# Gated mix of two attentions on one core: another order of the first loads, splits and keys, and borrowed probability buffers kept until the 48th quad

## The chip, the cores and the metric

One core of one Trainium2 chip. The metric is device microseconds of one execution, the median of the runs shown; lower is better. The inputs lie in the chip's memory at the start and the result must lie there at the end.

## The reference

The input x has 2048 tokens of width 512. Two attentions with 32 heads of width 16 are computed from it and mixed by a gate per token. In attention a all heads share one key and one value head; attention b has its own keys and values for each head. Cut to what matters:

```
g = sigmoid((x * gate_w).sum(-1))                      # one number per token
qa = heads(x @ wq); ka = x @ wk; va = x @ wv           # 32 query heads, one key and one value head
a = concat(softmax(qa @ ka.T * 16**-0.5) @ va) @ wo_a
qb, kb, vb = heads(x @ wqkv)                           # 32 heads each
b = concat(softmax(qb @ kb.T * 16**-0.5) @ vb) @ wo_b
out = g * a + (1 - g) * b
```

All is float32. The exponential is needed for 2 x 32 x 2048 x 2048 scores.

## The kernel before

**Tiles.** P = 128 partitions, NT = 16 token tiles of x, which are loaded two at a time as eight pairs (`x_tiles[k]`, k = 0 to 7; "x tile" below means such a pair). The heads of each attention are cut into NG = 4 groups of eight. The groups of a and b take turns (a0, b0, a1, b1, ...), and each group is done in two halves of the queries, each half in two parts of four heads: 32 phases in all. A phase has 32 *quads* of two *scores* each, one for each pair of its heads. So there are 1024 quads and 2048 scores; a score u = 2 x quad + 0 or 1 is a block of 128 x 1024 numbers. Scores 0 to 255 belong to group a0, 256 to 511 to b0, and so on.

**A score's way.** TensorE multiplies keys with queries into a PSUM bank named `sc` (eight matmuls, L623). ScalarE takes the exponential of the bank into a probability buffer in SBUF (L637, out `prob` or another borrowed name). TensorE multiplies the probabilities with the values and adds them up in the PSUM bank `pair[0]` (L678). Keys and queries are held as sums of two float16 numbers ("high part" and "residue"), so that the products keep float32's accuracy.

**Chained quads.** VectorE takes some quads from ScalarE: it computes the exponential by a polynomial, from the bank `pair[1]` (also called `spare`). Each such score is a chain of six instructions on VectorE: convert (L837), mantissa (L840), power (L844) and three steps of the polynomial (L849). Which quads are chained is the set `vector`.

**What sets the order.** The program is written out by a planner while it is built (`plan`): at each step it looks at estimated clocks of the engines (`plan.pe`, `plan.act`, `plan.dve`), at due times and at free buffers, and decides whether TensorE next does a score, a pair of values, or a piece of other work (a *unit*: x turns, products of queries, keys and values for the next group, output products). The estimates are constants at the top of the file, in nanoseconds: `EXP` = 904 for an exponential, `SCORES` = 215, `PRODUCT` = 215, and `X_JOB` = 560 for a quarter of one x tile's turns. A run then simply executes the order that came out; the planner's constants cost no time themselves, but another constant gives another order.

**Buffers.** Six probability buffers (`prob0` to `prob5`) are permanent. At the start the planner also has the SBUF of things that are done with or not needed yet: the first x tiles (`lent`), four buffers of the pool for group b's keys (`early0` to `early3`) and three in group b's value tile (`vB`), the last seven called `borrowed`. When the values of a quad are done, `summed` gives its two buffers back, except borrowed ones from the 16th quad on (`at[0]` is the quad that the next score belongs to):

```
for tile in (probs[2 * m], probs[2 * m + 1]):                          # L687
    if id(tile) in borrowed and at[0] >= 16:                           # L688
        continue
```

**The start.** Before the planner takes over, the work is written by hand. x tiles 0 and 1 are loaded over SyncE's and ScalarE's queues, 2 and 3 over SyncE's, then the query weights (`wqa`) over ScalarE's and behind them three small loads (`gate_w`, `wk`, `wv`, into the buffer `prob`, L289). For each of x tiles 0 to 3, TensorE turns the tile (`x_turns`, L298), ScalarE writes the high part (`x_hi`, L312) and VectorE the residue (`x_lo`, L317) into `xT`. The query weights are split in the same way (`first_w`, L248 on ScalarE and L249 on VectorE), the small weights in two steps on VectorE (`split`, L219 and L220); for each, SyncE's queue then moves a copy with its two halves of 64 rows swapped (`swapped`, L212). The loop before:

```
for k in range(4):                                                     # L1143
    if k == 3:
        banks.append(bank(2))
    x_turns(k, banks[k], TURNS)
    x_hi(k, as_x(banks[k]), nc.scalar)
    if k == 0:
        first_w()
        split(wkv16[0][:, 0], wkv16[0][:, 1], wkv, UP)
        ...
    x_lo(k, as_x(banks[k]))
```

The four x tiles have three banks of their own and `spare`; the first and the fourth share one (`bank(2)` takes the place that the first had). After the loop come the products of the first key tile (`kv_products`, L332, and `halve`, L351 to L356, which split them into high part and residue), then the query products Q of group a0 (L1163), whose high part ScalarE takes (L1167) and whose residue VectorE takes (L1172), and which sixteen transfers (`lay`, L401), eight of them ahead of the first score, move to the tiles `Qa`. The keys are turned by TensorE (`k_turn`, L367) and copied by VectorE into `kA` (`k_put`, L377). Then follow the other key tiles, x tile 4 and the first scores; x tiles 5 to 7 and the other keys come between scores.

## Time and profile before

| | |
|---|---|
| median of 3 runs | 1838.48 us (1838.03 to 1838.57) |
| the profiled execution's own time | 1836.4 us |
| its span | 1834.6 us |
| busy share of the span: TensorE (PE) | 95% |
| ScalarE (ACT) | 97% |
| VectorE (DVE) | 71% |
| GpSimd (POOL) | 16% |
| matmuls | 45161 |
| first exponential starts | 27.96 us |
| last exponential starts | 1811.77 us |

Times within an execution are microseconds from the start of the span. The profile names engines PE, PEld (TensorE's weight loads), DVE, ACT, POOL and SP; a "q" behind a name is the queue on which that engine issues DMAs. In a row of the page's groups stand the line, the engine, the operation, what it writes <- what it reads, the count of instructions, then the busy time and the mean nanoseconds of one, then the engine's idle time just ahead of these instructions with what released it. A row of the timeline begins with its start and duration; a bracket at the end holds how long the engine idled ahead of it, and on what. A row of windows has the window and its length, then the busy time with the count of instructions (of one line on its engine, or, where all are asked for, of PE, PEld, DVE, ACT and POOL in this order), and in the last columns the granted TensorE clock, the share of the DMA engines that was busy (over 1 where several packets overlap), and GB/s.

### The profile page before, as it was taken

The page shows a single profiled execution, that of the slowest core. Times are in us where ns is not written, and L with a number is a line of the kernel's source. Part 1 is how long each engine was busy: PE and PEld are TensorE (multiplying, and loading weights), DVE is VectorE, ACT ScalarE, POOL GpSimd, SP SyncE. Part 2 cuts the span into 40 slices and gives each one's busy share as a digit, 9 for nine tenths or more (in the row PEclk, how much of TensorE's full clock was granted, in tenths as well). Part 3 has the DMA queues.
Part 4 walks back from the last instruction along what each step waited for, and adds up shares of the span by engine and source line. Part 5 has one row for each costly group of instructions (what it writes and reads, how often), then busy time and mean ns, then how long its engine had stood idle before and what let it go on. Part 6 is the DMA issues. An engine that isn't in the chain of part 4 may idle for free.

```text
span 1834.6 us, 96600 instructions
## 1 busy us (share of the span) xinstructions
PE 1746.1 (95%) x45161; PEld 847.5 (46%) x45161; DVE 1300.5 (71%) x1465; ACT 1786.2 (97%) x1948; POOL 291.9 (16%) x367
## 2 busy tenths in 40 slices
PE   8999999999999999998999999999999999999896
PEld 5544444444444444444444444444444444444442
DVE  5277656789565776869667656886967567588886
ACT  5999999999999999999999999999999999999995
POOL 2212002121020121311202012132200202112000
PEclk9999999999999999999999999999999999999998
DMA  5121122233131232411313112342211213235211
GB/s 151 36 61 44 51 54 61 77 71 55 32 76 39 55 66 59 89 43 34 55 43 73 32 41 57 78 83 60 50 39 43 55 38 70 54 58 135 49 61 61
DMA packets 64887, 109.45 MB, mean 60 GB/s; under 512 B 14480, under 2 KB 22928, under 8 KB 64480
## 3 DMA queue, kind: packets, MB, share of 16 engines
q0 software_dynamic: 21504, 43.99, 13.0%
q1 hardware_dynamic: 39744, 56.99, 11.2%
q8 instruction: 355, 5.82, 1.3%
q10 hardware_dynamic: 3232, 2.23, 0.4%
q14 instruction: 52, 0.43, 0.1%
HBM read 14.75 MB, written 33.55 MB: 26 GB/s over the span
## 4 chain that ended last, share of the span: by engine, by line
ACT 73%; PE 11%; issue 8%; DVE 7%; DMA 1%; SPq 0%; ACTq 0%; DVEq 0%; POOL 0%
ACT prob L637 73%; PE pair L678 5%; PE sc L623 3%; DVE vec L849 2%; PE pair L207 1%; DVE vec L837 1%; DVE vec L844 1%; DVE sum L517 1%; DVE vec L840 0%; DVE dT L568 0%; PE pair L298 0%; SPq L561 0%; PE pair L1163 0%; PE pair L332 0%; DMA vec<-in_A_x_dram 0%
## 5 line engine op out<-in xcount | busy, mean ns | idle before, releaser
L637 ACT ACTIVATE prob<-sc 128x1024 f32<-128x1024 f32 x1911 | 1757.5, 1127 | 9.2 <-PE sc L623 8.6
L678 PE MATMUL pair<-prob,vA 64*32 64x512 f32 (+1 forms) x8016 | 515.6, 570 | 0.1
L678 PE MATMUL pair<-prob,vB 64*32 64x512 f32 (+1 forms) x7840 | 509.1, 578 | 0.0
L623 PE MATMUL sc<-Qb,K 64*32 64x512 f16 x7632 | 400.4, 380 | 42.8 <-ACT prob L637 32.1
L849 DVE SCALAR_TENSOR_TENSOR vec<-vec,vec 128x1024 f32<-128x1024 f32 x348 | 424.2, 1232 | 3.5
L623 PE MATMUL sc<-Qa,kA 64*32 64x512 f16 x7824 | 406.0, 380 | 17.7 <-ACT prob L637 9.5
L623 PEld LDWEIGHTS <-K 64*32 64x32 f16 x8192 | 201.2, 89 | 421.5 <-issue 383.1
L623 PEld LDWEIGHTS <-kA 64*32 64x32 f16 x8192 | 199.6, 89 | 387.9 <-issue 344.6
L837 DVE TENSOR_SCALAR vec<-pair 128x1024 int32<-128x1024 f32 x116 | 140.9, 1215 | 59.2 <-PE pair L623 59.0
L678 PEld LDWEIGHTS pair<-prob,vA 64*32 64x32 f32 x8016 | 154.9, 105 | 21.3 <-issue 3.1
L678 PEld LDWEIGHTS pair<-prob,vB 64*32 64x32 f32 x7840 | 151.7, 105 | 18.2 <-issue 0.5
L849 DVE SCALAR_TENSOR_TENSOR vec<-vec 128x1024 f32<-128x1024 f32 x116 | 143.3, 1236 | 1.1
L527 POOL DMA_DIRECT2D out_dram<-sum x48 | 60.0, 1250 | 386.4 <-DVE sum L517 359.8
L568 DVE RECIPROCAL dT<-dT 128x256 f32<-128x256 f32 (+1 forms) x66 | 111.4, 1693 | 9.7 <-DMA dT<-raw 9.7
L743 DVE COPY raw<-pair 128x1024 f32<-128x1024 f32 x31 | 37.9, 1222 | 96.8 <-PE pair L678 96.8
L517 DVE TENSOR_SCALAR sum<-pair,gate_up 128x512 f32<-128x512 f32 x112 | 77.7, 735 | 29.4 <-PE pair L207 29.3
L840 DVE TENSOR_SCALAR vec<-vec 128x1024 int32<-128x1024 int32 x116 | 84.5, 728 | 1.6
L844 DVE TENSOR_SCALAR vec<-vec 128x1024 int32<-128x1024 int32 x116 | 85.5, 737 | 0.0
L442 DVE TENSOR_SCALAR hivb<-pair 128x1024 f16<-128x1024 f32 x8 | 9.8, 1225 | 98.3 <-PE pair L207 98.3
L442 DVE TENSOR_SCALAR hiqb<-pair 128x1024 f16<-128x1024 f32 x8 | 9.8, 1225 | 92.0 <-PE pair L207 92.0
L401 POOL DMA_DIRECT2D Qa<-hiqa x31 | 17.6, 568 | 349.9 <-DVE hiqa L442 329.2
L207 PEld LDWEIGHTS <-o 64*32 64x32 f16 x3072 | 51.5, 93 | 39.1 <-ACT o L574 5.7
(160 smaller groups left out, 1253.3 us busy)
## 6 DMA issues: line engine op xcount, KB each, us to landing
out_dram<-sum POOLq DMA_DIRECT2D x48, 512.0 KB, 5.7
vB<-vB SPq DMA_DIRECT2D x16, 384.0 KB, 4.1
dT<-raw SPq DMA_DIRECT2D x32, 128.0 KB, 3.5
oT<-raw SPq DMA_DIRECT2D x32, 128.0 KB, 3.6
out_dram<-sum SPq DMA_DIRECT2D x8, 512.0 KB, 3.3
xT<-out_dram SPq DMA_DIRECT2D x16, 256.0 KB, 4.3
dT<-raw SPq DMA_DIRECT2D x62, 64.0 KB, 2.2
out_dram<-xT SPq DMA_DIRECT2D x12, 256.0 KB, 2.5
```

The source lines that it names most:

```text
L207: nc.tensor.matmul(outs[n : n + COLS, i], lhs[i][rows(i), n : n + COLS], rhs[i][rows(i)], start=start, stop=stop)
L517: nc.vector.tensor_scalar(state["sum"][:, e], pair[1][:, e], g, None, op0=ALU.mult)
L527: done = plan.on_pool([lambda: nc.gpsimd.dma_start(dst, state["sum"], accum_op=ALU.add)], t, 1300)
L568: nc.vector.reciprocal(d[:, c : c + cut], d[:, c : c + cut])
L623: nc.tensor.matmul(bank[a : a + COLS, hh], k[rows(hh), key : key + COLS], Q[src, gi, half, p][rows(hh), j * BLK : (j + 1) * BLK], start=Tr ...
L637: nc.scalar.activation(probs[u], sc, AF.Exp, scale=SCALE / (UP * UP))
L678: nc.tensor.matmul(pair[0][32 * k : 32 * k + 32, i, cols], v[rows(i)], probs[2 * m + k // 2][rows(i), hh, cols], start=first, stop=last)
L743: nc.vector.tensor_copy(state["raw"], full)
L837: nc.vector.tensor_scalar(tile("p").bitcast(I32), pair[1], SCALE / (UP * UP) / math.log(2) * 2.0 ** 23, None, op0=ALU.mult)
L840: nc.vector.tensor_scalar(tile("m").bitcast(I32), tiles["p"].bitcast(I32), 0x7FFFFF, 125 << 23, op0=ALU.bitwise_and, op1=ALU.bitwise_or)
L844: nc.vector.tensor_scalar(tile("w").bitcast(I32), tiles["p"].bitcast(I32), 0x7F800000, 0x40000000 | LEAD, op0=ALU.bitwise_and, op1=ALU.bit ...
L849: nc.vector.scalar_tensor_tensor(p, m if i == 3 else p, VEC[i], m if i else w, op0=ALU.add, op1=ALU.mult)
```

## The change

It has three parts. In the start, ScalarE loads its exponential table ahead of issuing anything else, and the three small loads are issued on GpSimd's queue; each x tile's residue is computed directly behind its high part, with the query weights' split behind the first tile's and the small weights' split behind the second's; all key products come behind Q's, and the copy of the first turned keys is on ScalarE. Borrowed buffers are used until the 48th quad instead of the 16th. And the planner counts 685 ns instead of 560 for a quarter of an x tile's turns.

```diff
@@ constants
-X_JOB = 560
+X_JOB = 685
@@ loads of the small weights
+    nc.scalar.activation(warm, warm, AF.Exp)
     for src, m in parts_kv:
-        nc.scalar.dma_start(wkv[:, :, m], src)
-    nc.scalar.activation(warm, warm, AF.Exp)
+        nc.gpsimd.dma_start(wkv[:, :, m], src)
     nc.vector.memset(stats, 0.0)
     nc.gpsimd.memset(vA[0], 1.0)
     nc.gpsimd.memset(vA[1], 1.0)
@@ copies of turned keys
-    def k_put(h, bank, tiles):
+    def k_put(h, bank, tiles, copy=nc.vector.tensor_copy):
...
-            nc.vector.tensor_copy(to, bank.rearrange("p a q -> p (a q)")[:, at * P : (at + n) * P])
+            copy(to, bank.rearrange("p a q -> p (a q)")[:, at * P : (at + n) * P])
@@ summed
-            if id(tile) in borrowed and at[0] >= 16:
+            if id(tile) in borrowed and at[0] >= 48:
                 continue
@@ start
         x_turns(k, banks[k], TURNS)
         x_hi(k, as_x(banks[k]), nc.scalar)
+        x_lo(k, as_x(banks[k]))
         if k == 0:
             first_w()
+        if k == 1:
             split(wkv16[0][:, 0], wkv16[0][:, 1], wkv, UP)
             swapped(wkv16[1], wkv16[0], nc.sync)
             for i in range(2):
                 x_load(4, i, nc.sync)
-        x_lo(k, as_x(banks[k]))
...
     kn, take, halve, k_top = kv_split(0, pv)
-    kv_products(0, 0, pv, STEPS)
-    halve(slice(0, 1))
     for n, (c, w, a, b) in enumerate(STEPS):
...
     for i in range(2):
         nc.scalar.activation(hilo[0][:, i], spare[:, i], AF.Copy, scale=UP ** -1)
-    turned_k = bank(3)
-    k_turn(kn, turned_k, (0, 4))
-    k_put(0, turned_k, (0, 4))
+    kv_products(0, 0, pv, STEPS)
+    halve(slice(0, 1))
     for i in range(2):
         nc.vector.scalar_tensor_tensor(hilo[1][:, i], spare[:, i], UP ** -1, hilo[0][:, i], op0=ALU.mult, op1=ALU.subtract)
     to = q_tiles("a", 0, 0)
-    moves = ... ((nc.sync, nc.scalar), (nc.gpsimd, nc.sync, nc.gpsimd, nc.scalar)) ...
+    moves = ... ((nc.sync, nc.scalar), (nc.gpsimd, nc.sync, nc.scalar, nc.gpsimd)) ...
     for move in moves[0][:2] + moves[1][:2] + moves[0][2:] + moves[1][2:]:
         move()
-    for i in range(1, 4):
+    kv_products(0, 1, pv, STEPS)
+    turned_k = bank(3)
+    k_turn(kn, turned_k, (0, 4))
+    k_put(0, turned_k, (0, 4), nc.scalar.copy)
+    for i in range(2, 4):
         kv_products(0, i, pv, STEPS)
     halve(slice(1, 4))
     last = bank(4)
```

What the planner makes of it shows at two places. First the start. On ScalarE, the difference of the two orders (a minus is the kernel before, a plus the changed one), with the loads of x and the query weights ahead and the first tile's high part (L312) and the query weights' (L248) behind:

```order
 L238 DMA wqa_133<-in_A_wq_dram 128x4x128
-L289 DMA prob_102<-in_gate_w_dram 128x4x1
-L289 DMA prob_102<-in_A_wk_dram 128x4x16
-L289 DMA prob_102<-in_A_wv_dram 128x4x16
-L290 ACT_TABLE_LOAD
-L290 ACTIVATE warm<-warm 128x1
+L288 ACT_TABLE_LOAD
+L288 ACTIVATE warm<-warm 128x1
 L312 ACTIVATE xT<-pt_146 128x8x128
 L248 ACTIVATE w16qa_135<-wqa_133 128x512
```

The three small loads have left ScalarE's queue, and the table's load has moved up behind the query weights' DMA.

On VectorE at the same place: `pt_146`, `pt_147`, `pair_83` and `pt_223` are the banks of x tiles 0 to 3, `w16qa` the split query weights, `wkv` the split small weights.

```order
 L1142 CAST ident_86<-ident 128x128
+L317 SCALAR_TENSOR_TENSOR xT<-pt_146,xT 128x8x128
 L249 SCALAR_TENSOR_TENSOR w16qa_135<-wqa_133,w16qa_135 128x512
+L317 SCALAR_TENSOR_TENSOR xT<-pt_147,xT 128x8x128
 L219 TENSOR_SCALAR wkv_93<-prob_102 128x132
 L220 SCALAR_TENSOR_TENSOR wkv_93<-prob_102,wkv_93 128x132
-L317 SCALAR_TENSOR_TENSOR xT<-pt_146,xT 128x8x128
-L317 SCALAR_TENSOR_TENSOR xT<-pt_147,xT 128x8x128
 L317 SCALAR_TENSOR_TENSOR xT<-pair_83,xT 128x8x128
 L317 SCALAR_TENSOR_TENSOR xT<-pt_223,xT 128x8x128
```

The residues of the first two x tiles have moved ahead of the small weights' split, the first also ahead of the query weights'.

Second, the end of group b0, scores 503 to 513. On ScalarE of the kernel before (the number behind `sc` is that of the score, the number behind that a running one):

```order
L637 ACTIVATE prob3_100<-sc503_11506 128x1024
L637 ACTIVATE prob1_98<-sc504_11524 128x1024
L637 ACTIVATE prob4_101<-sc505_11543 128x1024
L637 ACTIVATE prob2_99<-sc512_11561 128x1024
L637 ACTIVATE prob3_100<-sc513_11580 128x1024
```

And of the changed kernel:

```order
L637 ACTIVATE prob5_102<-sc505_11335 128x1024
L637 ACTIVATE prob3_100<-sc506_11354 128x1024
L637 ACTIVATE prob4_101<-sc507_11428 128x1024
L637 ACTIVATE prob0_97<-sc512_11446 128x1024
L637 ACTIVATE prob5_102<-sc513_11520 128x1024
```

Before, the scores 506 to 511 are not on ScalarE but chained on VectorE; in the changed order 506 and 507 are exponentials. In the same way 188 and 189, chained before, are exponentials in the changed order; over the whole program 1936 scores stand on ScalarE instead of 1932. From score 503 to about score 1243 each engine of the changed kernel has the rows that stand 512 scores later in the kernel before, and from there to the end it has the same rows at the same score. VectorE of the changed kernel, around score 520 (`raw7` is the copy of a phase's value sums, L475 prepares values of the next group b):

```order
L743 COPY raw7_11551<-pair1_83 128x1024
L475 TENSOR_SCALAR vB0_91<-pair0_82 128x8x2x16
L837 TENSOR_SCALAR vec0_103<-pair0_82 128x1024
L840 TENSOR_SCALAR vec2_105<-vec0_103 128x1024
L844 TENSOR_SCALAR vec1_104<-vec0_103 128x1024
L837 TENSOR_SCALAR vec3_106<-pair0_82 128x1024
L849 SCALAR_TENSOR_TENSOR vec0_103<-vec2_105 128x1024
```

VectorE of the kernel before, around score 1032:

```order
L743 COPY raw15_22069<-pair0_82 128x1024
L475 TENSOR_SCALAR vB0_91<-pair1_83 128x8x2x16
L837 TENSOR_SCALAR vec0_103<-pair1_83 128x1024
L840 TENSOR_SCALAR vec5_108<-vec0_103 128x1024
L844 TENSOR_SCALAR vec3_106<-vec0_103 128x1024
L837 TENSOR_SCALAR vec1_104<-pair1_83 128x1024
L849 SCALAR_TENSOR_TENSOR vec0_103<-vec5_108 128x1024
```

The kinds and their order are the same, with the two PSUM pairs and some scratch buffers exchanged.

2 lines of the change are left out of this document (1 added, 1 removed).

## The prediction

> **What bounds the kernel now.** I read the page first, then the activations by stretches, then the first 28 us.
>
> ```profile
> span 1834.6 us, 96600 instructions
> PE 1746.1 (95%) x45161; PEld 847.5 (46%) x45161; DVE 1300.5 (71%) x1465; ACT 1786.2 (97%) x1948; POOL 291.9 (16%) x367
> ACT 73%; PE 11%; issue 8%; DVE 7%; DMA 1%; SPq 0%; ACTq 0%; DVEq 0%; POOL 0%
> L637 ACT ACTIVATE prob<-sc 128x1024 f32<-128x1024 f32 x1911 | 1757.5, 1127 | 9.2 <-PE sc L623 8.6
> ```
>
> ScalarE's exponentials (L637) are 73% of the chain that ended last, and once they run ScalarE idles for only some 9 us. So the time is: when the first exponential starts, how many there are times their pace, what ScalarE waits in between, and the tail. The windows of line L637 give the pace and the stretches. I cut them at scores 32, 503 and 1243 (the second and third cut are explained below); the activation's place follows from counting the score numbers in ScalarE's order. Each count but the first and the one that starts at 27.95 holds one activation that began ahead of the window.
>
> ```profile
> 27.95:477.10 449.15, 446.01 (x485) 1.00 0.22 55
> 477.10:1120.09 642.99, 639.82 (x697) 1.00 0.26 56
> 920.51:1565.48 644.97, 641.95 (x699) 1.00 0.25 55
> 1120.09:1811.77 691.68, 689.44 (x751) 1.00 0.27 59
> 27.95:58.96 31.01, 30.12 (x32) 1.00 0.24 65
> 58.96:477.10 418.14, 415.89 (x454) 1.00 0.21 54
> 592.53:704.42 111.89, 111.89 (x123) 1.00 0.25 53
> ```
>
> 592.53 to 704.42 has no idle time: 122 activations in 111.89 us, **0.917 us each**. That is what one exponential more or less on ScalarE costs. At this pace the first 32 would take 29.3 us and took 31.0, so 1.7 were lost; the next 453 would take 415.4 and took 418.1, so 2.7 were lost.
>
> **The count.** The page's groups L637 hold 1932 activations; 116 of the 2048 scores go to VectorE (line L837). In ScalarE's order of the changed kernel 1936 scores stand: VectorE has two fewer in the third phase (188 and 189 move to ScalarE) and two fewer in the eighth (506 and 507). So ScalarE gets 4 x 0.917 = 3.67 us more. Two of these can be read as a measured stretch. From score 503 on, the changed kernel does on TensorE, score by score, what the kernel before does 512 scores (one pair of head groups) later, as far as score 1243; from there to the end it does what the kernel before does at the same score. The kernel before took 644.97 us for 1015 to 1755 and 642.99 us for 503 to 1243, waits included: **+1.98 us**. From 1243 on nothing changes: **0**. The scores before 503 are in new order, with two more activations: **+1.83 us**, and their waits are open.
>
> **The beginning.** In the timeline's rows (start, duration, engine, line) ScalarE first, its DMA queue ACTq with it:
>
> ```profile
> 1.66 0.46 ACTq L238 DMA_DIRECT2D wqa<-in_A_wq_dram  x1
> 6.45 1.28 ACT L290 ACT_TABLE_LOAD   x1 [6.45 <-DMA vec<-in_A_x_dram]
> 7.85 1.01 ACT L312 ACTIVATE xT<-pt 128x1024 f16<-128x1024 f32 x1
> 8.76 0.62 ACT L248 ACTIVATE w16qa<-wqa 128x512 f16<-128x512 f32 x1
> 14.46 1.02 ACT L312 ACTIVATE xT<-pt 128x1024 f16<-128x1024 f32 x1 [2.73 <-PE pt L298]
> 20.93 1.08 ACT L1167 ACTIVATE hiqa<-pair 128x512 f16<-128x512 f32 x2 [5.44 <-PE pair L1163]
> 23.37 1.40 ACTq L401 DMA_DIRECT2D Qa<-loqa  x2
> 27.96 1.02 ACT L637 ACTIVATE prob<-sc 128x1024 f32<-128x1024 f32 x1 [1.47 <-PE sc L623]
> ```
>
> VectorE:
>
> ```profile
> 9.41 0.69 DVE L249 SCALAR_TENSOR_TENSOR w16qa<-wqa,w16qa 128x512 f16<-128x512 f32 x1 [4.00 <-ACT w16qa L248]
> 10.70 0.23 DVE L219 TENSOR_SCALAR wkv<-prob 128x132 f16<-128x132 f32 x1 [0.60 <-DMA prob<-in_A_wv_dram]
> 11.18 2.35 DVE L317 SCALAR_TENSOR_TENSOR xT<-pt,xT 128x1024 f16<-128x1024 f32 x2
> 16.66 0.18 DVE L351 TENSOR_SCALAR k<-pair 128x32 f32<-128x32 f32 x1
> 17.11 0.23 DVE L356 TENSOR_TENSOR kn<-k,kn 128x64 f16<-128x64 f32 x1
> 22.05 1.29 DVE L1172 SCALAR_TENSOR_TENSOR loqa<-pair,hiqa 128x512 f16<-128x512 f32 x2 [0.39 <-ACT hiqa L1167]
> 25.79 1.02 DVE L377 CAST kA<-pt 128x384 f16<-128x384 f32 x2 [1.29 <-PE pt L367]
> 27.00 1.22 DVE L317 SCALAR_TENSOR_TENSOR xT<-pt,xT 128x1024 f16<-128x1024 f32 x1
> ```
>
> TensorE, and SyncE's queue:
>
> ```profile
> 5.20 3.71 PE L298 MATMUL pt<-ident,vec 128*64 128x128 f32 x64 [0.38 <-DVE ident L1141]
> 8.75 1.92 PE L298 MATMUL pair<-ident,vec 128*64 128x128 f32 x32
> 12.45 1.97 PE L298 MATMUL pt<-ident,vec 128*64 128x128 f32 x32 [1.79 <-DVE xT L317]
> 14.35 0.77 PE L332 MATMUL pair<-wkv,xT 64*128 64x33 f16 x48
> 15.54 5.36 PE L1163 MATMUL pair<-xT,w16qa 64*128 64x512 f16 x48 [0.42 <-ACT xT L312]
> 20.83 0.30 PE L367 MATMUL pt<-ident,kn 128*64 128x128 f16 x4
> 25.25 0.51 PE L367 MATMUL pt<-ident,kn 128*64 128x128 f16 x12
> 27.48 0.41 PE L623 MATMUL sc<-Qa,kA 64*32 64x512 f16 x8 [1.73 <-DMA Qa<-loqa]
> 10.13 1.21 SPq L212 DMA_DIRECT2D w16qa<-w16qa  x2
> ```
>
> And how long such a swap of a weight's rows takes to land, from the DMA issues (kilobytes each, median us):
>
> ```profile
> w16qa<-w16qa POOLq DMA_DIRECT2D x6, 128.0 KB, 2.4
> ```
>
> The stall to see is TensorE's: the fourth tile's turns, at 12.45, wait 1.79 us for the bank of the first tile, whose residue stands on VectorE (11.18) behind weights that came by DMA at 10.70. Now step by step. ScalarE loads its table at 2.1 instead of 6.45, so the first tile's high part starts when its turns end (half of 5.20 to 8.91, so 7.1) and ends at 8.1. Its residue is first on VectorE: 8.1 to 9.3 (half of 2.35). The weights' residue follows at 9.5 to 10.2; in the kernel before it ended at 10.1, so their swap leaves at the same time, by 10.13 + 1.21 = 11.3, and at 2.4 has landed by 13.7. The fourth tile's turns start when TensorE is free, 8.75 + 1.92 = 10.7, and end at 12.65; its high part on ScalarE ends at 13.7. **The Q products start at 13.7, not 15.54: -1.8**, and end at 19.1. The swap has no room left there; it did land by 15.5 before, since Q waited for L312 and not for a DMA.
>
> Then some is given back. The first tile of keys (0.77), which stood in a gap at 14.35, now runs behind Q, 19.1 to 19.9. Its halving on VectorE (16.66 to 17.34, 0.68) lands between Q and Q's residue: 20.0 to 20.6, then the residue to 21.9, against 23.34. TensorE from 19.9: three more key tiles at 0.77, the turn (0.30), the fifth x tile (1.97) and the other keys' turn (0.51), 25.0 in all against 25.76. These keys' copy on VectorE (1.02) ends at 26.1, and the first score follows at 26.2, against 27.48. Q's residue is no longer last: its moves took from 23.37 to the first score in 27.48, at most 4.1, and 21.9 + 4.1 = 26.0. The second score uses the bank of the fifth x tile, whose residue (1.22, behind the keys' copy, the values and the gate) ended at 28.22 and now ends at 27.5; the second exponential moves from 28.89 to 28.0. I take **-0.85 us** from there, not -1.25 from the first score, since the later one holds.
>
> What is hidden: the keys' copy that moves to ScalarE stands behind Q's moves (1.40, from 21.9 to 23.3) and costs between 0.5 and the 1.08 of L1167; it is done by 24.4, before the bank is turned into again at 24.5. Without that cover it costs what it is late. The three small loads on GpSimd's queue are the first thing there and push two memsets that nobody reads before 26 us. Nothing before Q's last third needs the small weights' split; in VectorE's order it stands ahead of the residues of the third and fourth tile. That third starts at 13.7 + 3.6 = 17.3, two residues take 2.45, so the weights may land at 14.3 instead of 10.7 for nothing.
>
> The first 32 scores lost 1.7 us since TensorE has x turns, key products and values between scores. In the changed order the same work (12 turn jobs, 8 key jobs, 8 pairs of values) stands between 30 scores instead of 28, up to the second keys' turn. A code fetch of TensorE falls in it as well:
>
> ```profile
> 49.23 0.27 PE L332 MATMUL pair<-wkv,xT 64*128 64x33 f16 x8 [0.66 <-issue]
> ```
>
> Two more scores give ScalarE 1.83 us of work there and cost TensorE 2 x 0.41: up to -1.0, with another fetch +0.3. I take **-0.5**.
>
> **The other waits before score 503.** They lost 2.7 us; the largest is of this kind, TensorE at a chained pair's values before VectorE has finished it:
>
> ```profile
> 341.39 2.96 ACT L637 ACTIVATE prob<-sc 128x1024 f32<-128x1024 f32 x3 [1.09 <-PE sc L623]
> ```
>
> Before, those values stood 10 scores behind their products (9.2 us), with 9.2 us of VectorE work ahead of them. The changed order has that place no more, but one with 18 scores (16.5 us) and 16.6 us of work, at score 408. One goes, one comes: **0**, between -1.9 (none) and +2.6 (two more). Keeping the borrowed tiles only moves values later; the last borrowed tile is filled at score 110, and keys are laid there behind score 194, so no queue waits for it.
>
> **The sum.** 1834.6 - 0.85 - 0.5 + 1.83 + 1.98 + 0 = 1837.1, so +2.5 us. The profiled execution's own time was 1836.4 and the median of the runs 1838.48; on the median the forecast is **1840.9 us**. 0.2% (about what a measurement of this kernel can tell from no change) is 3.7 us: faster means under 1834.8, slower over 1842.2.
>
> **The rivals.**
> *A wait that takes the place of the one removed (slower).* The pair at score 408 and the next tight one, at 458 (18 scores, 15.7 us of work), can both make TensorE wait as at 341 us. So can group b's second keys: their last products now stand behind score 276 (before: 250), they are needed at 288, and I work out some 3 us in hand. Then ScalarE loses 1.3 us more for each: one gives 1842.2, two 1843.5. It decides from one more such wait than before. For it: the whole first quarter is new order. Against: the three places have 0 to 3 us in hand. Chance 0.22.
> *The start gives nothing (slower).* The loads are crowded:
>
> ```profile
> 8.00:9.00 1.00, 1.00 (x24) 1.00 (x22) 0.00 (x0) 1.00 (x2) 0.00 (x0) 1.00 1.15 270
> ```
>
> The DMA engines are full. In the kernel before, the small weights were sent behind x and Q's weights; now they are sent among them. At worst Q's weights land when the last small load did, 10.6 instead of 8.7: ScalarE splits them until 11.2, their swap leaves at 11.9 and Q starts 1.1 later. The start is then +0.25, the time 1842.0. [...] Chance 0.10.
> *ScalarE's waits go (no change).* More buffers in the first 96 scores let TensorE run ahead: -1.9 more, 1839.0. It would have to come from waits that are not for buffers (the row at 341 us isn't). Chance 0.10.
> *The four exponentials cost nothing,* where TensorE and not ScalarE is last: 1837.2. Against: the windows show 0.917 in every quiet stretch, and the two for 503 to 1243 are measured. Chance 0.05.
>
> **How the numbers follow.** The forecast has 0.53. The range takes the ends of start, first scores and waits as far as they go together: low 1838.0 (-1.0 in the first 32, -1.9 in waits, and the start as taken), high 1843.8 (two more waits and a start 0.6 worse). Slower over 0.2%: most of the first rival, half of the second and the upper end of the forecast, 0.31. Faster by 0.2% would need 6.1 us beyond the forecast, more than all waits that the changed part has (1.7 + 2.7): 0.03. Within: 0.66.
>
> **What would show it.** The changed profile should show L637 in 1936 activations, the first at 26.7 and the second at 28.0; Q's products at 13.7 with no wait of TensorE for L317 at 12.45; the 33rd activation at about 57.6 (58.97 before); and from score 503 to 1243 some 645 us, from there to the last 691.7. Wrong is the forecast if score 503 starts later than 478.5 or earlier than 475.5 (477.1 - 1.35 + 1.83 = 477.6), or if the later stretches differ by over 1 us from these.

## The result, and the profile after

The changed kernel takes 1844.24 us (median of 7 runs, 1842.63 to 1845.91) against 1838.03 for the kernel before on the same chip; the ratio is **1.0029, 95% interval 1.0020 to 1.0039**, which is +5.3 us where +2.4 was forecast (1840.9 against 1838.48). In a second set of runs it was 1.0036 (1.0022 to 1.0050). The profiled execution took 1845.78 us, its span is 1844.0. That is one of the slower executions of this kernel, as 1836.4 was one of the faster ones of the kernel before, so the two profiles are 9.4 us apart where the medians are 6.2 apart.

The windows of the exponentials' line (L637), cut at the same scores as before (the first exponential, 32, 503, 1243, the last):

```profile
31.30:63.51 32.21, 29.82 (x32) 1.00 0.28 75
63.51:484.23 420.72, 418.10 (x457) 1.00 0.21 53
484.23:1129.44 645.21, 641.66 (x699) 1.00 0.26 55
1129.44:1820.84 691.40, 689.09 (x752) 1.00 0.28 59
```

From score 503 on it is as forecast: 645.21 us to score 1243 ("some 645") and 691.40 from there to the last (691.7). Of the 9.4 us, 3.3 are there at the first exponential (31.30 against 27.96), 1.2 come in the first 32 scores (32.21 against 31.01), 2.6 from there to score 503 and 2.2 to score 1243; behind it -0.3 to the last exponential and +0.3 in the tail. The start was forecast as a gain. VectorE's first instructions, in the kernel before:

```profile
1.31 1.47 DVE L271 TENSOR_SCALAR index<-index 128x1 f16<-128x1 f16 x7
4.86 0.29 DVE L1141 TENSOR_TENSOR ident<-pair,index 128x128 f32<-128x128 f32 x1 [1.94 <-PE pair L1140]
```

And in the changed kernel, with GpSimd's rows of the same time below:

```profile
1.31 3.64 DVE L271 TENSOR_SCALAR index<-index 128x1 f16<-128x1 f16 x7
7.47 0.29 DVE L1141 TENSOR_TENSOR ident<-pair,index 128x128 f32<-128x128 f32 x1 [2.38 <-PE pair L1140]
1.27 0.94 POOL L290 DMA_DIRECT2D prob<-in_gate_w_dram  x1 [0.83 <-POOLq L1446]
2.20 0.77 POOL L290 DMA_DIRECT2D prob<-in_A_wk_dram  x1
2.96 0.75 POOL L290 DMA_DIRECT2D prob<-in_A_wv_dram  x1
```

L271 is a chain of seven tiny instructions that count 0 to 127 into `index`, from which the identity for the turns (L1141) is made. They took 1.47 us and now take 3.64, while GpSimd prepares the three small loads (until 3.7) and then does the two memsets that the loads pushed back (0.54 us each, until 4.7). The third to sixth of the seven take 0.46, 1.05, 0.42 and 0.99 us, where 0.17 is usual. The identity is 2.6 us later. The prediction does not have these rows: it looked at what the loads do to other loads, and not at what VectorE does while GpSimd prepares them.

TensorE from there to the first score, and ScalarE's first exponentials:

```profile
5.01 0.29 PE L1138 MATMUL pair<-level,index 128*128 128x128 f16 x1 [2.37 <-DVE index L271]
7.82 5.26 PE L298 MATMUL pt<-ident,vec 128*64 128x128 f32 x64 [0.38 <-DVE ident L1141]
14.66 1.91 PE L298 MATMUL pt<-ident,vec 128*64 128x128 f32 x32
17.70 5.36 PE L1162 MATMUL pair<-xT,w16qa 64*128 64x512 f16 x48 [1.12 <-ACT xT L312]
26.90 0.57 PE L332 MATMUL pair<-wkv,xT 64*128 64x33 f16 x31 [1.03 <-issue]
27.40 1.97 PE L298 MATMUL pt<-ident,vec 128*64 128x128 f32 x32
30.81 0.41 PE L623 MATMUL sc<-Qa,kA 64*32 64x512 f16 x8 [1.12 <-DVE kA L377]
31.30 1.02 ACT L637 ACTIVATE prob<-sc 128x1024 f32<-128x1024 f32 x1 [0.86 <-PE sc L623]
32.69 3.81 ACT L637 ACTIVATE prob<-sc 128x1024 f32<-128x1024 f32 x4 [0.37 <-PE sc L623]
```

The fourth tile's turns (14.66) follow without the wait of 1.79 us, as forecast. But TensorE idled 2.37 us for the index, and then took 5.26 us for the first two tiles instead of 3.71. In windows of TensorE (length, busy time, count, granted clock):

```profile
7.82:11.02 3.20, 3.20 (x30) 1.00 0.67 202
11.02:13.08 2.06, 2.06 (x42) 1.00 0.00 0
```

The same matmuls run at 0.107 us apiece until 11.02 and at 0.054 from there (38 of the 42 start in the second window). The record of the granted clock begins with a rise to full at 11.02, and at 4.24 in the kernel before; the clock column reads 1.00 ahead of its first record, so the half clock of a start is seen in the counts and not in that column. Q starts at 17.70, not at 13.7: of these 4.0 us some 2.6 are the identity's and 1.5 the clock's. Behind Q, at 26.90, TensorE waits 1.03 us for nothing that the rows show, in the middle of the key products. I take it for a wait for TensorE's own code: in all fourteen profiles listed below, each such wait of 0.5 us or more in the first 60 us ends 2.3 to 2.7 us behind the start of a 16 KB transfer on the instruction queue (here one that starts at 24.39; in the kernel before one at 46.90, ahead of the wait of 0.66 that ends at 49.23).

### The profile page after: what moved, and what is told of

It reads as the page before. It is cut to its first block, busy times and chain, and to the rows that moved or that the text cites. A ratio compares the mean times of both kernels' runs of the same rounds, so it can differ in the third digit from the quotient of the medians.

```text
span 1844.0 us, 96547 instructions
## 1 busy us (share of the span) xinstructions
PE 1750.1 (95%) x45145; PEld 847.1 (46%) x45145; DVE 1273.8 (69%) x1435; ACT 1790.3 (97%) x1954; POOL 295.8 (16%) x370
## 3 DMA queue, kind: packets, MB, share of 16 engines
q0 software_dynamic: 21600, 44.06, 13.5%
q1 hardware_dynamic: 39744, 56.99, 11.1%
## 5 line engine op out<-in xcount | busy, mean ns | idle before, releaser
L637 ACT ACTIVATE prob<-sc 128x1024 f32<-128x1024 f32 x1874 | 1728.3, 1126 | 9.8 <-PE sc L623 8.7
L678 PE MATMUL pair<-prob,vA 64*32 64x512 f32 (+1 forms) x7664 | 505.5, 571 | 0.1
L849 DVE SCALAR_TENSOR_TENSOR vec<-vec,vec 128x1024 f32<-128x1024 f32 x336 | 413.4, 1242 | 3.2
L837 DVE TENSOR_SCALAR vec<-pair 128x1024 int32<-128x1024 f32 x112 | 135.6, 1211 | 58.2 <-PE pair L623 58.0
L678 PEld LDWEIGHTS pair<-prob,vA 64*32 64x32 f32 x7664 | 151.1, 105 | 18.4 <-issue 1.4
L840 DVE TENSOR_SCALAR vec<-vec 128x1024 int32<-128x1024 int32 x112 | 81.1, 724 | 1.3
L844 DVE TENSOR_SCALAR vec<-vec 128x1024 int32<-128x1024 int32 x112 | 80.0, 714 | 0.0
```

The lines of the kernel that those rows point to most:

```text
L637: nc.scalar.activation(probs[u], sc, AF.Exp, scale=SCALE / (UP * UP))
L678: nc.tensor.matmul(pair[0][32 * k : 32 * k + 32, i, cols], v[rows(i)], probs[2 * m + k // 2][rows(i), hh, cols], start=first, stop=last)
L837: nc.vector.tensor_scalar(tile("p").bitcast(I32), pair[1], SCALE / (UP * UP) / math.log(2) * 2.0 ** 23, None, op0=ALU.mult)
L840: nc.vector.tensor_scalar(tile("m").bitcast(I32), tiles["p"].bitcast(I32), 0x7FFFFF, 125 << 23, op0=ALU.bitwise_and, op1=ALU.bitwise_or)
L844: nc.vector.tensor_scalar(tile("w").bitcast(I32), tiles["p"].bitcast(I32), 0x7F800000, 0x40000000 | LEAD, op0=ALU.bitwise_and, op1=ALU.bit ...
L849: nc.vector.scalar_tensor_tensor(p, m if i == 3 else p, VEC[i], m if i else w, op0=ALU.add, op1=ALU.mult)
```

## The experiments

Each table row is one profiled execution and the ratio of the runs to those of the kernel before on the same chip; the last column is from the start of score 32's exponential to the end of the span.

| kernel | ratio (95%) | Q starts | first exponential | score 32 | from 32 to the end |
|---|---|---|---|---|---|
| before | 1 | 15.54 | 27.96 | 58.97 | 1775.7 |
| changed | 1.0029 (1.0020-1.0039) | 17.70 | 31.30 | 63.51 | 1780.5 |
| changed again (e12) | 1.0036 (1.0022-1.0050) | 16.59 | 31.57 | 65.95 | 1775.8 |
| e1 changed, small loads on ScalarE | 1.0007 (0.9998-1.0016) | 14.58 | 29.63 | 61.50 | 1775.8 |
| e2 before, small loads on GpSimd | 1.0010 (1.0001-1.0019) | 18.63 | 30.83 | 63.33 | 1775.8 |
| e3 before, planner's two settings | 1.0003 (0.9994-1.0012) | 15.45 | 28.16 | 63.48 | 1776.7 |
| e4 new start, loads on ScalarE, old order | 1.0007 (0.9998-1.0016) | 13.82 | 27.73 | 58.71 | 1774.4 |
| e5 changed, TensorE kept busy | 1.0045 (1.0032-1.0058) | 15.45 | 30.54 | 63.13 | 1776.9 |
| e6 changed, index in PSUM | 1.0031 (1.0020-1.0043) | 15.53 | 32.30 | 64.39 | 1776.4 |
| e7 before, TensorE filled | 1.0001 (0.9992-1.0010) | 15.54 | 27.65 | 58.44 | 1773.0 |
| e8 as e4, second keys split | 1.0015 (1.0007-1.0024) | 15.77 | 32.62 | 63.73 | 1775.0 |
| e9 as e4, x tiles 6 and 7 later | 1.0002 (0.9993-1.0011) | 14.88 | 28.02 | 60.57 | 1775.2 |
| e10 before, residues first | 0.9999 (0.9990-1.0008) | 16.87 | 29.47 | 61.83 | 1776.1 |
| e11 changed, loads late | 1.0033 (1.0023-1.0043) | 15.89 | 31.19 | 62.97 | 1777.1 |

**e1: the small loads back on ScalarE's queue.**

```diff
-        nc.gpsimd.dma_start(wkv[:, :, m], src)
+        nc.scalar.dma_start(wkv[:, :, m], src)
```

> The changed kernel, with only the three small loads back on ScalarE's queue (behind the table load). Theory G (the loads on GpSimd's queue hold up VectorE's seven index instructions, 3.64 us instead of 1.47, and TensorE, idle for 2.4 us meanwhile, then turns its first tile at half its pace, 1.5 us more): the index chain takes 1.5 us again, the identity is done by 5.2 instead of 7.8, Q's products start at 13.5 instead of 17.7, the first exponential at 27.1 instead of 31.3, and the time is 4.2 us below the changed kernel's, near 1.0006 of the kernel before. Rival D (the small loads are late or crowd the DMA engines, and VectorE's chain was slow for another reason): the chain stays at 3.6 us and the time within 1 us of the changed kernel's, 1.0029. Rival K (the other order of keys and Q costs the start): the chain is short, but the first exponential is still after 29.5.

The chain and the turns of the fifth x tile, in the timeline:

```profile
1.31 1.46 DVE L271 TENSOR_SCALAR index<-index 128x1 f16<-128x1 f16 x7
24.17 3.53 PE L298 MATMUL pt<-ident,vec 128*64 128x128 f32 x32
```

The chain is back at 1.46 us, and the time falls from 1.0029 to 1.0007, by some 4 us, as theory G has it; rival D's 1.0029 is outside the interval. Q starts at 14.58, though not at 13.5, because the first tiles were turned at half clock for a while here too (4.32 us for the first two, 3.71 in the kernel before). The first exponential is at 29.63, 2.5 late: the fifth tile took 3.53 us instead of 1.97. That fulfils rival K's number (after 29.5), though by a half clock (0.50 from 23.99 to 27.41 us) that e4, with the same order of keys and Q, does not have (1.97 us for the fifth tile); e12 takes it up.

**e2: only the small loads on GpSimd's queue, in the kernel before.** The edit of e1 the other way round.

> The kernel before, with only the three small loads moved to GpSimd's queue. Theory G: VectorE's index chain takes 3.6 us instead of 1.47, the identity is done 2.6 us later, the first tile's turns take 3.5 us instead of 1.8; the small weights no longer hold up the first tile's residue, which gives back about 1.2, so Q's products start at 18.5 instead of 15.5 and the time is 3 us more (1.0016). Rival D: the chain stays at 1.5 us; Q's products start at 14.5 to 15.5 and the time is the same or 1 us less.

```profile
1.31 3.64 DVE L271 TENSOR_SCALAR index<-index 128x1 f16<-128x1 f16 x7
18.63 5.34 PE L1163 MATMUL pair<-xT,w16qa 64*128 64x512 f16 x48
30.36 0.41 PE L623 MATMUL sc<-Qa,kA 64*32 64x512 f16 x8 [1.83 <-DMA Qa<-loqa]
```

Chain, Q and the first score (30.36, 2.9 late) are where theory G put them, and D's are not. The runs show +0.10%, 1.8 us (0.2 to 3.5), where 3 was expected: the same sign, less than half of what e1 gave back.

**e3: only the planner's two settings.**

```diff
-X_JOB = 560
+X_JOB = 685
-            if id(tile) in borrowed and at[0] >= 16:
+            if id(tile) in borrowed and at[0] >= 48:
```

> The kernel before, with only the two settings of the planner changed (685 for a quarter of x turns, borrowed buffers until the 48th quad): the order behind the first scores is then that of the changed kernel, with 1936 exponentials, and the start that of the kernel before. Theory P (four more exponentials at 0.917, and the waits of the new order about as large as those of the old): +3.7 us with the first exponential at 28.0, so 1.0020, score 503 at 479 to 480 and 645 us from there to score 1243. Rival S (the four cost nothing, the start alone makes the difference): within 1 us of the kernel before.

The runs lie at 1.0003 (0.9994 to 1.0012), nearer to theory S than to P, whose 1.0020 is outside: +0.6 us, at most 2.2. e1 and e4, which differ in the same two settings, are both at 1.0007. In the profile the first 32 scores took 35.3 us (31.0 in the kernel before), with half clock from 29.3 to 32.7 and from 53.2 to 60.0 us; a start that varies so much can cover the settings' own share. The last column of the table leaves the start out. Seven of the profiles have the changed order behind it and seven the old one, and their means are 1777.0 and 1775.0 (within 4.7 and 3.1 us): **+2.0 us net**, 0.4 to 3.6 by their scatter, where 3.8 was forecast. By stretch, it is +1.1 from 32 to 503 (forecast 1.83), +1.6 to 1243 (forecast 1.98) and -0.7 behind it (forecast 0). The exponentials themselves cost what was forecast: in the first two stretches ScalarE is busy for 1.9 and 1.8 us more, and 2 x 0.917 is 1.83. But it idles 0.8 and 0.2 us less there. The last stretch has the same rows in both orders, so I take its -0.7 for scatter.

**e4: the new start with the loads on ScalarE, planner's settings as before.** The edit of e1, and e3's undone.

> The start of the changed kernel with the small loads on ScalarE's queue, and the two settings of the planner as before: 1932 exponentials, and TensorE's order behind the first score that of the kernel before. Theories G and P: the first exponential at 27.0 and the second at 28.0 to 28.3, the rest as before: 0.9 us less than the kernel before (0.9995). Rival K (the other order of keys and Q costs the start): first exponential after 29, 1.0005 or more.

```profile
13.82 5.36 PE L1162 MATMUL pair<-xT,w16qa 64*128 64x512 f16 x48 [1.12 <-ACT xT L312]
23.33 0.57 PE L332 MATMUL pair<-wkv,xT 64*128 64x33 f16 x31 [1.33 <-issue]
23.82 1.97 PE L298 MATMUL pt<-ident,vec 128*64 128x128 f32 x32
27.73 1.02 ACT L637 ACTIVATE prob<-sc 128x1024 f32<-128x1024 f32 x1 [0.86 <-PE sc L623]
29.12 4.74 ACT L637 ACTIVATE prob<-sc 128x1024 f32<-128x1024 f32 x5 [0.37 <-PE sc L623]
```

Without GpSimd's part, Q starts where the prediction had it (13.82 for 13.7). All of the 1.7 us are gone by the second exponential, 29.12 against 28.89 before and 28.0 forecast: the 1.1 us too much are about the wait of 1.33 among the key products, for the second exponential comes 1.4 behind the first, and 1.3 was forecast. The ratio, 1.0007, is no gain. Rival K is right about the time and wrong about the place: the first exponential isn't late.

**e5: TensorE kept busy while the index is made.**

```diff
-    for n in range(3):
+    for n in range(9):
         nc.tensor.matmul(pv[:, 0], kA[:, :P], kA[:, :BLK], start=True, stop=True)
```

> The changed kernel with nine instead of three matmuls on zeros ahead of the index matmul, so that TensorE doesn't idle from 2.65 to 5.0 us while VectorE's index chain is held up. Theory G's second half (the idle TensorE loses its granted clock and turns the first tile at half pace): the chain stays at 3.6 us; the five matmuls behind the index take 1.1 to 1.9 us instead of 2.3, the first two tiles' turns 3.7 to 4.3 instead of 5.26, Q's products start at 15.3 to 16.5 instead of 17.7, and the time is 1.2 to 2.4 us below the changed kernel's: 1.0016 to 1.0023. Rival (the slow turns come from x arriving late or from DMA traffic): the turns stay at 5.2 us and the time at 1.0029.

```profile
1.18 3.56 PE L1137 MATMUL pair<-kA 128*128 128x512 f16 x9 [1.18 <-DVE kA L266]
5.08 1.24 PE L1140 MATMUL pair<-kA 128*128 128x512 f16 x5
6.70 3.71 PE L298 MATMUL pt<-ident,vec 128*64 128x128 f32 x64 [0.38 <-DVE ident L1141]
10.91 0.63 ACT L248 ACTIVATE w16qa<-wqa 128x512 f16<-128x512 f32 x1 [1.17 <-DMA wqa<-in_A_wq_dram]
```

The half clock's part is shown: with TensorE busy, the clock is full at 4.14, the five matmuls take 1.24 us instead of 2.34, and the first two tiles 3.71 instead of 5.26. The last row is a cost that lay hidden under the late identity: Q's weights (`wqa`) land at 10.9, and ScalarE waits 1.17 us for them. Q starts at 15.45, within the expectation. The time does not follow: 1.0045, outside the expected 1.0016 to 1.0023 and above the changed kernel's interval (its own is 1.0032 to 1.0058).

**e6: the index counted in PSUM.**

```diff
-    nc.vector.memset(index[:, 0:1], 0.0)
+    count = pair[1][:, 0, :P]
+    nc.vector.memset(count[:, 0:1], 0.0)
     for n in (1, 2, 4, 8, 16, 32, 64):
-        nc.vector.tensor_scalar(index[:, n : 2 * n], index[:, :n], float(n), None, op0=ALU.add)
+        nc.vector.tensor_scalar(count[:, n : 2 * n], count[:, :n], float(n), None, op0=ALU.add)
+    nc.vector.tensor_copy(index, count)
```

> The changed kernel with the three small loads still on GpSimd's queue, but VectorE's seven index instructions work on PSUM in float32 and one copy at the end writes the index to SBUF. Theory G as a lock (GpSimd, while it prepares DMAs, holds a way to SBUF that these VectorE instructions need too): the seven instructions take 1.2 to 1.8 us, the copy waits at most until 3.7, the identity is done at 5.2 to 6.2 instead of 7.8, and the time is 1.6 to 4 us below the changed kernel's: 1.0007 to 1.0020. Rival (VectorE is slowed in general while GpSimd prepares DMAs, whatever it reads): the chain stays at 3 us or more and the time at 1.0029.

VectorE, and beside it GpSimd at the same loads as in the changed kernel:

```profile
1.37 1.50 DVE L272 TENSOR_SCALAR pair<-pair 128x1 f32<-128x1 f32 x7
2.90 0.29 DVE L273 CAST index<-pair 128x128 f16<-128x128 f32 x1
3.17 0.17 DVE L293 MEMSET stats<- 128x128 f32 x1
1.26 0.94 POOL L292 DMA_DIRECT2D prob<-in_gate_w_dram  x1 [0.83 <-POOLq L1448]
2.20 0.77 POOL L292 DMA_DIRECT2D prob<-in_A_wk_dram  x1
2.96 0.75 POOL L292 DMA_DIRECT2D prob<-in_A_wv_dram  x1
10.99 0.63 ACT L248 ACTIVATE w16qa<-wqa 128x512 f16<-128x512 f32 x1 [1.09 <-DMA wqa<-in_A_wq_dram]
```

The same seven instructions, in float32 on PSUM, run in 1.50 us straight through GpSimd's preparation. So VectorE isn't slow in general then. Its copy from PSUM to the index in SBUF (0.29 us) and its memset in SBUF (0.17) run through as well, so it isn't kept from SBUF altogether: held up are, in the changed kernel, the float16 instructions that read from SBUF and write to it (four of the seven take 0.42 to 1.05 us instead of 0.17). This run changed the place and the number format together, so which of the two matters is open. The traces show for how long VectorE is held up, 3.64 us for 1.47, and not by what means: the way to SBUF that the expectation supposes is in none of them. Q's weights are late again (1.09 us wait), Q starts at 15.53, and again the time, 1.0031, does not follow.

**e11: the small loads still on GpSimd, but late.** Fourteen memsets ahead of them.

```diff
+    for n in range(14):
+        nc.gpsimd.memset(vA[n % 2], 1.0)
     for src, m in parts_kv:
         nc.gpsimd.dma_start(wkv[:, :, m], src)
```

> The changed kernel with the three small loads still on GpSimd's queue, but fourteen memsets of 0.53 us ahead of them (to buffers that are set to the same value later), so that they are issued at 8 us and later. Theory G with its second cost (the loads hold up VectorE's index chain, and share the DMA engines with x and Q's weights, so that these land at 10.9 instead of 8.8 in the two runs that freed the chain): the chain takes 1.5 us, Q's weights land before 9, Q's products start at 13.6 to 14.6, and the time falls from 1.0029 to 1.0005 to 1.0012. Rival (what costs is that these loads go through GpSimd at all): 1.002 or more with Q's products before 14.6. If GpSimd's preparation holds up VectorE's residues at 8 to 11 us instead, Q starts at 15 to 16 and the time is 1.0015 to 1.002.

```profile
1.32 2.88 DVE L271 TENSOR_SCALAR index<-index 128x1 f16<-128x1 f16 x7
0.74 6.69 POOL L290 MEMSET vA<- 128x512 f32 x14 [0.29 <-POOLq L1448]
10.50 0.62 ACT L248 ACTIVATE w16qa<-wqa 128x512 f16<-128x512 f32 x1
```

A miss in its design: GpSimd's memsets hold the chain up too (2.88 us). What it does show is that Q's weights are not waited for when the small loads leave at 7.4. Q starts at 15.89, and the time is 1.0033, above all that was expected with such a Q (1.0015 to 1.002): it is no cure.

**e7: the kernel before, with TensorE filled where it waits for Q's transfers.**

```diff
     k_turn(kn, turned_k, rest)
+    for n in range(6):
+        nc.tensor.matmul(spare[:, 0], xT[:, 0, 0, 0, :P], xT[:, 0, 0, 0, :BLK], start=True, stop=True)
```

> The kernel before with six matmuls whose result nobody reads, where TensorE waits for Q's transfers ahead of the first score (1.7 us). Theory C (the half clock that single executions show between 24 and 35 us, 1 to 2 us each, comes from TensorE's idle time just before): no half clock between 26 and 36 us, the first 32 scores in 31.0 us, and the median 0.5 to 1 us lower (0.9995 to 0.9997). Rival: such half clocks come whatever TensorE does, and the time is the same or 0.2 us more.

No half clock in its profile (a granted clock of 1.00 from 22 to 30 us), score 32 at 58.44 and the shortest span of all (1831.4 us); the ratio, 1.0001 (0.9992 to 1.0010), shows no gain. Theory C isn't refuted by it and isn't shown.

**e8: e4 with the second keys copied half by ScalarE, and four such matmuls.**

```diff
-    k_put(0, turned_k, rest)
+    k_put(0, turned_k, rest[:3], nc.scalar.copy)
+    nc.vector.tensor_copy(kA[:, 5 * P : 8 * P], turned_k...[:, 3 * P : 6 * P])
```

> The start of the changed kernel with the small loads on ScalarE's queue and the planner's old settings, and the second turned keys copied half by ScalarE and half by VectorE, with four matmuls whose result nobody reads while TensorE waits for them. The first score of that start waited for VectorE's key copies (1.02) and the second for the fifth x tile's residue behind them (1.22): both should come 0.5 us sooner, the first exponential at 27.2 and the second at 28.6, and the time 0.5 us below that of the same start without the split, 0.9995 to 1.0003. If the first exponential stays at 27.7 or later, ScalarE's half is the later one.

```profile
25.95 0.56 PE L332 MATMUL pair<-wkv,xT 64*128 64x33 f16 x31 [2.01 <-issue]
26.45 3.61 PE L298 MATMUL pt<-ident,vec 128*64 128x128 f32 x32
32.14 0.41 PE L623 MATMUL sc<-Qa,kA 64*32 64x512 f16 x8 [0.78 <-DVE kA L1192]
```

The wait for the copies fell from 1.12 to 0.78, but here the wait among the key products was 2.01 and the fifth tile was turned at half clock; the first exponential came at 32.62 and the ratio was 1.0015. A miss.

**e9: e4 with the loads of x tiles 6 and 7 behind Q's moves.**

```diff
-    for k in range(5, 8):
-        for i in range(2):
-            x_load(k, i, nc.sync)
+    for i in range(2):
+        x_load(5, i, nc.sync)
...
     for move in moves[0][:2] + moves[1][:2] + moves[0][2:] + moves[1][2:]:
         move()
+    for k in range(6, 8):
+        for i in range(2):
+            x_load(k, i, nc.sync)
```

> The start of the changed kernel with the small loads on ScalarE's queue and the planner's old settings (1932 exponentials), and the loads of x tiles 6 and 7 issued behind Q's moves instead of ahead of Q. Theory F (TensorE's code for the key products behind Q waits in the DMA engines behind the loads of x tiles 4 to 7, so that a Q that ends earlier gains nothing): with two of these four tiles out of the way the loads end near 18.5, the code arrives by 19.5 to 20.5, the key products run without the stall of 0.9 to 2.0 us that all six profiles of this start show, the first exponential is at 26.4 to 26.9 instead of 27.73 and the time 0.8 us below that of the same start without this edit, 0.9998 to 1.0006. Rival (the code is late for its own reason): stall of 0.9 us or more at the key products, first exponential at 27.5 or later. If x tile 6 lands late, TensorE waits for it between scores near 31 us and gives the gain back there.

```profile
23.62 0.57 PE L332 MATMUL pair<-wkv,xT 64*128 64x33 f16 x31 [0.57 <-issue]
24.12 1.97 PE L298 MATMUL pt<-ident,vec 128*64 128x128 f32 x32
27.54 0.41 PE L623 MATMUL sc<-Qa,kA 64*32 64x512 f16 x8 [1.12 <-DVE kA L377]
```

The wait shrinks to 0.57 us, below all others of this start (0.88 to 2.01), and from Q to the first score it takes 12.66 us (13.42 in e4). So other loads may be part of it, by this one profile, but it isn't gone, and the first exponential, at 28.02, missed the expected 26.4 to 26.9. The trace's transfers on the instruction queue (16 KB each) say more: the one in question starts 1.0 us behind the end of Q here and 1.3 to 2.3 behind it in the other eight profiles of this start, while with the first key tile ahead of Q it starts 0.3 to 1.9 us before Q ends (before, e2, e3, e7, e10). What sets its start, no run shows. Time 1.0002 (expected 0.9998 to 1.0006).

**e10: the kernel before with only the residues first.** The table load ahead, `x_lo` behind `x_hi`, the small weights' split at `k == 1`; loads, keys and settings as before.

> The kernel before with only these parts of the new start: the table load ahead, each x tile's residue behind its high part, the small weights' split behind the second tile. Loads on ScalarE's queue, first key tile ahead of Q, planner's settings as before. The fourth x tile's turns no longer wait (1.8 us before), the key product waits for the small weights' swap until 14 to 14.5, Q starts at 14.9 to 15.2 instead of 15.5. Theory F: Q ends only 0.4 us sooner, no code stall appears, the first exponential is at 27.4 to 27.7 and the time 0.3 us below the kernel before, 0.9996 to 1.0002. Rival (the residue order itself costs): first exponential after 28.2.

```profile
16.30 0.73 PE L332 MATMUL pair<-wkv,xT 64*128 64x33 f16 x45 [0.44 <-DMA wkv<-wkv]
22.38 1.99 PE L332 MATMUL pair<-wkv,xT 64*128 64x33 f16 x144
29.00 0.41 PE L623 MATMUL sc<-Qa,kA 64*32 64x512 f16 x8 [2.40 <-DMA Qa<-loqa]
```

With the first key tile ahead of Q, the 144 key products behind Q run through in 1.99 us without a wait: the long code wait belongs to the keys' new place (with the old place it is 0.3 us at most, in the kernel before). Q is no earlier (16.87), since the first tiles were turned at half clock until 9.22 (5.44 us for the first two) and the small weights, split later, are waited for (0.98 and 0.44 us). The first exponential, at 29.47, fulfils the rival's number (after 28.2), but the time, 0.9999, shows no cost of the residues' order.

**e12: the changed kernel once more.**

> The changed kernel itself once more, for a second profiled execution and more times. Theory G says what must be there in every execution: VectorE's index instructions from 1.3 to 5.0 us, the first turns at 7.8, TensorE's full clock not before 8 us, Q's products at 16.2 to 17.8. What the experiments so far left to chance is when the clock rises and whether it falls again between 23 and 36 us: without a fall the first exponential is near 31, with one near 32.5. From score 32 to the end 1776 to 1778.5 us, the mean of the five other profiles of this order being 1776.6 (the first profile of the changed kernel, 1780.5, would then be a late one). Time 1.0025 to 1.0040. Rival (the loads on GpSimd's queue slow the later part too): 1780 or more from score 32 to the end again.

VectorE's chain, the first turns (7.81), the late full clock (8.77) and Q (16.59) are where theory G put them. TensorE in three stretches of 3.41 us or less, in windows of its own (length, busy time, granted clock):

```profile
22.43:25.84 3.41, 2.25 (x140) 1.00 0.70 211
25.84:29.25 3.41, 3.41 (x59) 0.50 0.53 133
29.25:31.00 1.75, 0.72 (x18) 1.00 0.56 154
```

The clock is at half for 3.41 us, behind a stretch of the same length in which TensorE was busy for 66%. The fifth tile's turns and the keys' turn fall into it. Such a fall between 23 and 36 us is in six of the nine profiles of the new start and in three of five of the old; that, and when the clock first rises (4.1 to 11.1 us), can set two executions of one kernel some us apart before score 32 (63.51 and 65.95 in the two profiles of the changed kernel). From score 32 on it took 1775.8 us: the loads don't slow the later part, and 1780.5 was a slow throw. Why the clock falls, the trace does not show.

## Why the prediction was right in sign and short in size

It said slower by 2.4 us with no more than 0.31 for over 0.2%; it came out slower by 5.3, in the range of 1838.0 to 1843.8 on the median that the forecast stood on (1838.48 x 1.0029 = 1843.8), at its very end, and beyond the 0.2%. The changed kernel's own median, 1844.24, lies 0.4 above the range. (The ends that the prediction names for its range add up to 1838.5 and 1844.1, not to 1838.0 and 1843.8; no run shows the start 0.6 worse that its upper end has.) Its own sign of being wrong was met: score 503 started at 484.23, and 478.5 was the latest that it allowed.

That the forecast still had the sign is in part luck. The clear "slower" comes from a term that it had at nothing, the loads on GpSimd's queue: without it (e1) the same change is at 1.0007 (0.9998 to 1.0016), below the forecast's 1.0013 and not clear of no change.

*The count: right.* 1936 exponentials, and 645.21 and 691.40 us behind score 503, as read from before by shifting it 512 scores. Four exponentials cost ScalarE the 3.67 us of the sum (1.9 and 1.8 us of busy time, by fourteen profiles). The net is smaller, since less was lost in waits: 0.8 us less up to score 503, where the sum had no change and the third rival (ScalarE's waits go) had 1.9, and 0.2 from there to score 1243.

*The start: the step that failed.* "The three small loads on GpSimd's queue are the first thing there and push two memsets that nobody reads" costed them at nothing. They, and the memsets that they push, hold VectorE's index chain for 2.2 us and the identity for 2.6. Then TensorE stands idle (2.37 us) and turns the first tiles at half clock, 1.5 us in the first profile. So the term of -0.85 was +3.3 to +3.6 at the first exponential, and 3.8 to 4.1 at the second. Of the rivals, the first's times (1842.2 and 1843.5) came nearest, by another mechanism. The second's (1842.0) had a mechanism that was half real: Q's weights land at 10.9 and 11.0 (e5, e6), later than its 10.6, but the late identity hides that in the changed kernel.

*Behind Q: a second failed step.* "Then some is given back" had TensorE run from Q to the first score without a wait. With the loads on ScalarE (e4) Q starts at 13.82, the forecast's 13.7, and nothing is left of it at the second exponential, since a code wait sits in the moved key products (1.33 us in e4, 0.6 to 2.0 in the nine profiles of this start).

*The first 32 scores.* -0.5 was taken, with "another fetch +0.3". The first profile has +1.2, the second +3.4, with waits of TensorE at 57 us of 1.47 and 2.29 us, of the kind of a code wait:

```profile
58.81 0.59 PE L678 MATMUL pair<-early,vA 64*32 64x512 f32 x1 [1.47 <-issue]
```

Such gaps that begin between 46 and 58 us are 1.2 to 2.3 us long in six of the seven profiles of the changed order and no longer than 1.0 in any of the old one. They look like a part of what the planner's settings cost, some 1 us that the +2.0 from score 32 on doesn't hold (the first 32 scores take 32.9 us by the mean of the seven, 31.6 by that of the others); the forecast's +0.3 for "another fetch" was a third of it.

*Score 408.* The prediction's new tight place did stall, at score 409: from one exponential's start to the next it is 1.67 or 1.68 us in all seven profiles of the changed order, 0.75 above the pace (the rival had 1.3). The one at 458 did not. The first rival was right about one place, and the time did not need it, since the waits grew fewer in all.

**The sum as it came out.** By the runs: 1.3 us for the new start with the loads on ScalarE's queue (e4), nothing for the planner's settings on top of it (e1 against e4), and 4.0 for the loads on GpSimd's queue (the changed kernel against e1). Only the last is clear of noise, and in the kernel before the same loads cost 1.8 (e2). The profiles divide it otherwise, with 2 to 3 us for the planner's settings and nothing for the rest of the start; the two accounts don't agree, and fourteen single profiles are too few to decide.

**What stays open.** Moving the loads off GpSimd's queue gives back 0.22%, some 4 us (e1). But the kernels that shortened the chain or the half clock and kept the loads there (e5, e6, e11) gained nothing in the runs, though Q was 1.8 to 2.2 us earlier in their profiles than in the changed kernel's first (0.7 to 1.1 than in its second). In those profiles the gain goes between Q and the first score: 14.6, 16.1 and 14.8 us, where the changed kernel took 13.1 and 14.5, in code waits and half clock. Whether that must follow from an earlier Q or fell so by chance, five profiles can't say. So the chain, the late identity and the half clock are seen, but it is not shown that they make up the 4 us, nor how these divide between chain, clock and late weights; another cost of sending these loads over GpSimd's queue is not refuted. No version here is faster than the kernel before.

## What to carry to other kernels

A DMA issued on GpSimd was not free here, though GpSimd was idle: look at what VectorE does in SBUF while GpSimd prepares it, and at who waits for that, down to instructions of 0.2 us (seven of these took 3.64 us instead of 1.47, and the identity came 2.6 us later). A chain that is pulled forward by 1.7 us is worth that only if the next things, its code and its clock included, can come forward too (in e4 0.2 us of it was left at the first exponential). And one profiled execution of the start is one throw (score 32 at 63.51 and at 65.95 in two of the changed kernel): a difference of a few us needs the same stretch from several.

## What of the hardware was not expected

- With GpSimd preparing DMAs (0.75 to 0.94 us each), seven float16 instructions of VectorE from SBUF to SBUF took 3.64 us (the changed kernel, e2, e5, e12), and with GpSimd's memsets beside them (some 0.5 us each) 2.88 (e11); in the kernel before, where GpSimd is done at 1.7 us, they took 1.47. The same in float32 on PSUM, beside GpSimd's DMAs, took 1.50 (e6).
- TensorE's clock fell to half for 3.41 us (e12; 10.24 in e6) behind a stretch of 3.41 us in which it was 66% busy, on key products of 33 columns and waits (e12). In the nine profiles with such a fall, 1.0 to 2.3 us of that stretch were busy; in the kernel before, one with 1.7 us (24.7 to 28.1) had no fall behind it. So the busy share alone doesn't tell.
- With the small loads on GpSimd's queue from 1.3 us on, Q's weights landed 2 us later: at 10.9 in e5 and 11.0 in e6, and at 9.0 in e4 with these loads on ScalarE's queue from 4.8 on.
